# A decode step on one core: seven of V's eight chunks weighted on VectorE, the next queries ahead of its sums, the sum over V amid the next scores

## The chip, the cores and the metric

The kernel runs on 1 core of one Trainium2 chip. The core has a matrix engine (TensorE, PE in the profile), a vector engine (VectorE, DVE), a scalar engine (ScalarE, ACT), GpSimd (POOL) and SyncE (SP), which here only issues the transfers from the chip's main memory into the on-chip memory. TensorE writes to a separate memory of 8 banks (pS, pO and pK0 to pK5 in the code). The metric is the device time of one execution in microseconds, as the median over runs; less is better.

## The reference

Two kinds of layer alternate, attention over a cache (A) and a dense layer with GELU (B), for one query row `x` of 512 numbers, all in float32. The same caches and weights serve both passes.

```python
def _A_ref(x, k_cache, v_cache, wq, wo):            # H, Dh = 32, 128; 4096 keys
    q = (x @ wq).reshape(B, Sq, H, Dh).transpose(0, 2, 1, 3)
    scores = jnp.einsum("bhqd,bhkd->bhqk", q, k_cache) * (Dh ** -0.5)
    p = _softmax(scores, axis=-1)
    o = jnp.einsum("bhqk,bhkd->bhqd", p, v_cache)
    return o.transpose(0, 2, 1, 3).reshape(B, Sq, H * Dh) @ wo

def _B_ref(x, w1, b1, w2, b2):
    h = _gelu(jnp.einsum("bsd,df->bsf", x, w1) + b1)
    return jnp.einsum("bsf,fd->bsd", h, w2) + b2

x = x + _A_ref(_layernorm(x), k_cache, v_cache, wq, wo)
x = x + _B_ref(_layernorm(x), w1, b1, w2, b2)
x = x + _A_ref(_layernorm(x), k_cache, v_cache, wq, wo)
x = x + _B_ref(_layernorm(x), w1, b1, w2, b2)
```

## The kernel before, in words

The 32 heads are worked in G = 8 groups of J = 4 heads. Of one group, K and V are 8 MB each; both are cut into C = 8 chunks of 1 MB (one chunk is NC = 2048 numbers in each of 128 partitions, that is 512 for each of the four heads). The weights wq and wo of a group are 1 MB each and come as one transfer of 2 MB, the "pair" (wo of this group and wq of the next). The first pass goes through the groups 0 to 7; the second goes back from 6 (whose K and V, with 7's, are partly still on the chip) to 0. In the second pass the loop at L514 counts n from 2 to 7.

The on-chip memory holds one large tile, `arena`. Three "homes" of 8 MB each lie in it (A_AT, B_AT, C_AT); K and V of successive groups take them in turn, so that K of the next group goes where V of the group before lay, and V of the next group where K of this one lies. PAIR holds the pair, SCRATCH and TURNED short-lived results.

A group goes through these steps:

- `scores` (L222): for each chunk, four products of the queries z with K into pS, one for each head; each is two instructions in the profile, so a group's 32 products appear as x64.
- `exponentials` (L227): the maximum over pS (L228), the maximum over a head's rows through two small transposes (L230 to L233), the exponential on ScalarE (L237) with its sum.
- `weights` (L240): four transposes on TensorE, a copy to `pt` (L245), and the reciprocal of the sums (L251). `pt` and `rl` are the weights of V and 1 over their sum.
- V: `partly` (L407) lets TensorE take the first BY_PE = 3 chunks (`values`, L254, products into pO), and `weighted` (L261) lets VectorE take the other five: one multiplication of all five chunks by their weights in place (L265, 10240 numbers per partition), and additions that fold them onto one chunk (L270: 4096, 2048 and 2048 numbers).
- The next group's queries, `next_queries` (L379): the product of wq with x into pS, four transposes on VectorE (`turned`, L169), the queries z with the mean taken off (L218), and a memset of pS (L384).
- `group` (L393) begins with what the group before left "ahead": `sum_up` (L274) adds the folded chunk into pO by four products with ones, `head` (L278) picks the heads' results out of pO and scales them (L280, L284, L288). Then come this group's scores, and behind them `out_product` (L298), the product of the head with wo from PAIR into pO, which is added to the running sum of x behind the exponentials' first steps (`turned` at L404, `add_up` at L389).

Groups 0 to 5 of the first pass and n = 2 to 6 of the second give chunks to VectorE: 11 multiplications in all. In the last group of a pass, and in group 6 of the first, TensorE takes all eight chunks.

What sets the order: every transfer from SP, every product on TensorE, and the transposes on TensorE are pinned with `tc.keep_in_program_order`, so each of these queues runs in the order of the code. VectorE's instructions are not pinned; a planner places them when it takes them to be ready. SP issues, in order, K of a group, V, and the pair, and waits at each until the place that it writes has been read. So the pair waits for the product with wo of the group before, and K and V of the next group stand behind it. A few helpers record all instructions of a kind, so all loads have line L107 and all products L111; they are told apart by their tiles and shapes.

The mean of a layernorm is made by `minus_mean` (L189): a sum per partition is multiplied by a column of -1/512, in four products of 32 columns each, one for each quarter of the partitions. It is called twice (mean, variance) in each of the four layernorms. The dense layer (`mlp`, L307) streams w1 and w2 in pieces. In the last group of the second pass (L517 to L533) the code loads wo, w1 and w2 behind V; w1 goes to A_AT, where V of the group n = 6 lay.

Of the kernel before, what the change touches and what calls it, by code (L numbers as in the profile page):

```python
# [14 lines left out]
ALU = mybir.AluOpType  # L15
AX = mybir.AxisListType

P = 128
# [4 lines left out]
J = 4  # L23
C = 8
# [5 lines left out]
NC = 4 * U  # L30
# [13 lines left out]
TURNED = SHARED + 9 * U  # L44
ARENA = KEPT_K + 2 * U
HALVES = ((0, 4), (4, 8))
BY_PE = 3
ZQ = C - 1 + J * C
WIDE = 32 * J + 8 + 3 + 1
FRONT = 192  # L50
# [8 lines left out]
def decode_layers(ctx: ExitStack, tc: tile.TileContext, vectors, k, v, w, w1, w2, out):  # L59
    nc = tc.nc  # L60
# [21 lines left out]
    def small(name, n=1):  # L82
        nonlocal first_front, rest
        if name.startswith("gelu_"):
            i = "huaztg".index(name[-1])
            return cells[:, gelu + FB * i : gelu + FB * (i + 1)]
        if name not in places:
            fit = [j for j in range(J) if gaps[j] + n <= ends[j]]
            if name == "by_dma":
                places[name] = front, first_front, n  # L90
                first_front += n
            elif fit:
                places[name] = cells, gaps[fit[0]], n
                gaps[fit[0]] += n
            else:
                places[name] = cells, rest, n
                rest += n
        t, a, m = places[name]
        assert m == n and first_front <= FRONT and rest <= CELLS
        return t[:, a : a + n]  # L100

    def at(first, n):
        return arena[:, first : first + n]
# [6 lines left out]
    def matmul(*a, **kw):  # L110
        tc.keep_in_program_order(nc.tensor.matmul(*a, **kw))  # L111
# [10 lines left out]
    def by_four(t):  # L122
        return t.rearrange("p (j n) -> p j n", j=4)
# [10 lines left out]
    negmean = small("negmean")  # L134
# [8 lines left out]
    pS, pO = (psum.tile([P, 512], F32, name=n) for n in ("pS", "pO"))  # L143
# [19 lines left out]
    def turned(src, wide=False, to=None):  # L163

        t = turned_at[0] if to is None else to
        if wide:
            for j in range(J):
                q = slice(32 * j, 32 * j + 32)
                nc.vector.transpose(t[q], src[q, P * j : P * (j + 1)])  # L169
        else:  # L170
            nc.vector.transpose(t, src[:, :P])  # L171
        return t
# [14 lines left out]
        matmul(to[:, :n], zero[:, 0:1].to_broadcast([P, P]), at(of, n), start=not amid, stop=not amid)  # L187

    def minus_mean(s, at):  # L189
        for j in range(J):  # L190
            matmul(at[32 * j : 32 * j + 32, :], negmean.to_broadcast([P, 32]), s, start=True, stop=True)
        return at

    def mean_of(xs, s):
# [27 lines left out]
    def scores(z, c, kt):  # L222
        for j in range(J):
            matmul(pS[32 * j : 32 * j + C, :], z[:, C * j + C - 1 - c : C * j + 2 * C - 1 - c], kt[j],
                   start=(c == 0), stop=(c == C - 1))
# [32 lines left out]

    def weighted(pt, home):  # L261
        first = home + NC * BY_PE
        t = at(first, NC * (C - BY_PE)).rearrange("p (n d) -> p n d", d=P)
        w = pt.rearrange("p c j b -> p (c j b)")[:, 4 * J * BY_PE :]
        nc.vector.tensor_tensor(t, t, w.unsqueeze(2).to_broadcast([P, 4 * J * (C - BY_PE), P]), op=ALU.mult)  # L265
        n = C - BY_PE
        while n > 1:
            m = n // 2
            a, b = at(first + NC * (n - 2 * m), NC * m), at(first + NC * (n - m), NC * m)
            nc.vector.tensor_tensor(a, a, b, op=ALU.add)  # L270
            n -= m
        return quarters(first)

    def sum_up(t):  # L274
        for j in range(J):
            matmul(pO[32 * j : 32 * j + 4, :], one.to_broadcast([P, 4]), t[j], start=False, stop=True)

    def head(rl, last=False):  # L278
        ot = at(SCRATCH, U)
        nc.vector.transpose(ot, pO)  # L280
        o, on = small("o", 4), on_wide
        own = at(SCRATCH, 4 * 129).rearrange("p (b q) -> p b q", q=129)[:, :, :P]
        own = own.rearrange("p b (d q) -> p d b q", q=32)[:, :, :, 0]
        nc.vector.tensor_reduce(o, own, axis=AX.X, op=ALU.add)  # L284
        if last:
            nc.vector.tensor_scalar(on[:, :4], o, rl, None, op0=ALU.mult)
        else:
            nc.vector.tensor_scalar(in_quarters(on, 4), o.unsqueeze(1).to_broadcast([P, J, 4]), rl, None,  # L288
                                    op0=ALU.mult)
        return on  # L290
# [88 lines left out]
    def next_queries(xs, negm, wt, to=pO):  # L379
        for c in range(4):  # L380
            wide_query_block(to, c, xs, wt)
        z = queries(to, negm, wide=True)
        if to is pS:
            nc.vector.memset(pS, 0.0)  # L384
        return z
# [5 lines left out]


    def group(z, acc, ahead, k_blocks):  # L393
        if ahead:
            t, rl, wt = ahead
            sum_up(t)
            on = head(rl)
        for c, t in k_blocks:
            scores(z, c, t)
        if ahead:  # L400
            out_product(on, wt, pO)
        p = exponentials(sc, nsc)
        if ahead:
            acc = add_up(acc, of_32(turned(pO, wide=True), 4))  # L404
        return acc, *weights(p)

    def partly(pt, v_blocks, home):  # L407
        for c, t in v_blocks:
            if c < BY_PE:
                values(c, pt, t, c)  # L410
        return weighted(pt, home)


    negm, z, sc, nsc = first_queries(xs, s, wq_t, wide=True)
# [1 line left out]
    ahead = None  # L416
    for g in range(G):
        final = g == G - 1
        k_home, v_home = RING[2 * g % 3], RING[(2 * g + 1) % 3]
        acc, pt, rl = group(z, acc, ahead, blocks(k, g, k_home, HALVES if final else ((0, C),)))  # L420
        ahead = None
        if g == G - 2:
            nc.scalar.copy(at(KEPT_K, 2 * U), at(k_home + NC * C - 2 * U, 2 * U))
        if g < G - 2:
            t = partly(pt, blocks(v, g, v_home), v_home)
            pair = load(PAIR, of_w(g % 2, g, 2))
            ahead = t, rl, by_four(pair[:, :NC])
            z = next_queries(xs, negm, by_four(pair[:, NC:]), to=pS)
            continue
        for c, t in blocks(v, g, v_home, LAST if final else ((0, C),)):  # L430
            values(c, pt, t, c)
            if final and c in (5, 7):
                idle(pS)
            if g == G - 2:
                for j in range(J):
                    i = 4 * c + j - KEPT_V // U
                    if i >= 0:
                        nc.scalar.copy(pK[i], t[j])
        if final:
# [30 lines left out]
    xs, s = set_x(own, 0.5, xb)  # L470
# [4 lines left out]
    g = G - 2  # L475
# [12 lines left out]
    pair = load(C_AT + 24 * U, of_w(g % 2, g - 1, 2))  # L488
# [3 lines left out]
    p = exponentials(sc, nsc, lambda: queries(pO, negm, to=at(C_AT + 21 * U, P)))  # L492
    pt, rl = weights(p)
# [6 lines left out]
    for i, first in enumerate([SHARED, SHARED + U] + [PAIR + U * j for j in range(4)]):  # L500
        t = at(first, U)
# [4 lines left out]
    pt, rl = weights(exponentials(sc, nsc))  # L506
# [6 lines left out]
    homes, ahead = (A_AT, C_AT, B_AT), None  # L513
    for n in range(2, G):  # L514
        g, final = G - 1 - n, n == G - 1
        k_home, v_home = homes[(2 * n - 1) % 3], homes[2 * n % 3]
        acc, pt, rl = group(z, acc, ahead, blocks(k, g, k_home, HALVES if final else ((0, C),)))  # L517
        if not final:
            t = partly(pt, blocks(v, g, v_home, ((0, 6), (6, 8)) if n == 2 else ((0, C),)), v_home)
            pair = load(PAIR, of_w(g % 2, g - 1, 2))  # L520
            ahead = t, rl, by_four(pair[:, NC:])
            z = next_queries(xs, negm, by_four(pair[:, :NC]), to=pS)
            continue
        for c, t in blocks(v, g, v_home, LAST):
            values(c, pt, t, c)
            if c in (5, 7):
                idle(pS)
        wo_t = by_four(load(PAIR, of_w(g % 2, g, 1)))
        for a, b in W1_AT_END:
            load_w1(A_AT, a, b)  # L530
        for a, b in W2_AT_END:
            load_w2(A_AT + 11 * U, a, b)
        own = head_out(rl, wo_t, last=True)  # L533
# [46 lines left out]
```

## Time and profile before

| | |
|---|---|
| time, median of 3 runs | 672.79 us (672.41 to 673.16) |
| time of the profiled execution | 673.93 us |
| its span, from the first to the last instruction | 672.1 us |
| busy: PE / DVE / ACT | 400.7 / 329.1 / 22.8 us |
| the queue of the loads (q1) | 285.61 MB, 98.9% of 16 engines' span |
| mean granted clock of TensorE | 0.794 |

The profile is of one execution; what lies around its span, 1.8 us, is start and end of the program. In a row of the timeline stand the start in us, the duration in us, the engine, the line, the operation, the tile that it writes and the tile that it reads, a count where several were merged, and in brackets how long the engine had stood idle before it and what ended that. In a row of the groups stand the count, the busy time in us and the mean of one instruction in ns, then the idle time before them with what ended it. In a row of stretches stand the busy time of PE, of its weight load, of DVE, ACT and POOL, then the granted clock, the share of the DMA engines and GB/s. A merged row of DMA issues on SP covers the time from the first issue to the last; an issue does not tell when its data land, that shows at the instruction that waits for them.

### The profile page before, as it was taken

To read this page: it belongs to the slowest core of one execution; us is meant where nothing else is said; L and a number is where in the kernel's file an instruction comes from. 1 tells how busy PE (TensorE), PEld (TensorE's weight loads), DVE (VectorE), ACT (ScalarE), POOL (GpSimd) and SP (SyncE) were. 2 spreads that over 40 slices of the span, in tenths; PEclk is the share of its full clock that TensorE was granted. 3 is DMA by queue.
4 is the path that set the end of the run, shared out by engine and by line. 5 is a ranking of instruction groups with operands and counts; after the bars stand their busy time and mean duration, and the time that the engine had idled before them with its cause. 6 is when DMAs were issued, how large, how long until landed. Compare 5 with 4: busy or idle time off the path is not lost. (4 is left out here: it accounts for less than half of the span.)

```text
span 672.1 us, 5792 instructions
## 1 busy us (share of the span) xinstructions
PE 400.7 (60%) x2470; PEld 109.8 (16%) x2470; DVE 329.1 (49%) x480; ACT 22.8 (3%) x48; POOL 4.9 (1%) x23
## 2 busy tenths in 40 slices
PE   4543753647616556376767878728527466275685
PEld 1110210111201111011214222102102111021122
DVE  2059276393682945921121221492772936928521
ACT  0010000000000000002000110000000000000000
POOL 0000000000000000000000000000000000000000
PEclk9956765976769767677989999877758867687698
DMA  9999999999999999999999999999999999999996
GB/s 375 437 437 437 438 430 437 414 456 437 437 434 410 459 434 437 433 434 395 433 423 393 426 452 421 437 435 434 437 433 409 458 434 430 437 426 419 435 420 257
DMA packets 11258, 285.98 MB, mean 425 GB/s; under 512 B 1505, under 2 KB 1505, under 8 KB 3297
## 3 DMA queue, kind: packets, MB, share of 16 engines
q1 hardware_dynamic: 11088, 285.61, 98.9%
q8 instruction: 19, 0.31, 0.2%
q14 instruction: 7, 0.05, 0.0%
q10 hardware_dynamic: 144, 0.01, 0.0%
HBM read 285.62 MB, written 0.00 MB: 425 GB/s over the span
## 5 line engine op out<-in xcount | busy, mean ns | idle before, releaser
L111 PE MATMUL pO<-arena,cells 128*128 128x512 f32 (+4 forms) x376 | 93.0, 606 | 145.5 <-DVE arena L270 127.7
L111 PE MATMUL pS<-arena,front 128*8 128x512 f32 x1036 | 146.4, 706 | 32.8 <-DMA arena<-in_k 29.1
L265 DVE TENSOR_TENSOR arena<-arena 128x10240 f32<-128x10240 f32 x11 | 119.1, 10825 | 32.0 <-DMA arena<-in_v 31.8
L111 PE MATMUL pO<-arena 128*4 128x512 f32 x584 | 94.7, 806 | 44.7 <-DMA arena<-in_v 42.9
L270 DVE TENSOR_TENSOR arena<-arena 128x2048 f32<-128x2048 f32 (+1 forms) x33 | 98.5, 2985 | 0.7
L228 DVE TENSOR_REDUCE cells<-pS 128x1 f32<-128x512 f32 x16 | 11.1, 692 | 152.1 <-PE pS L111 152.1
L111 PEld LDWEIGHTS pO<-arena,cells 128*128 128x128 f32 (+3 forms) x376 | 28.2, 122 | 195.1 <-DVE arena L270 136.8
L111 PEld LDWEIGHTS pS<-arena,front 128*8 128x8 f32 x1036 | 31.4, 101 | 154.0 <-issue 110.3
L111 PE MATMUL pS<-arena,cells 128*1 128x128 f32 (+1 forms) x328 | 50.5, 384 | 8.5 <-DMA arena<-in_w 7.0
L280 DVE STREAM_TRANSPOSE arena<-pO 128x512 f32<-128x512 f32 x16 | 11.5, 717 | 54.1 <-PE pO L111 54.1
L242 PE MATMUL pO<-front,arena 128*128 128x128 f32 x64 | 12.8, 333 | 36.9 <-ACT arena L237 36.9
L111 PEld LDWEIGHTS pO<-arena 128*4 128x4 f32 x584 | 16.2, 102 | 107.7 <-issue 99.8
L169 DVE STREAM_TRANSPOSE arena<-pO 32x128 f32<-32x128 f32 x64 | 19.9, 311 | 20.1 <-PE pO L111 19.1
L237 ACT ACTIVATE arena<-pS,cells 128x512 f32<-128x512 f32 x16 | 12.4, 778 | 502.8 <-DVE cells L233 502.8
L111 PEld LDWEIGHTS pS<-arena,cells 128*1 128x1 f32 (+1 forms) x328 | 21.9, 118 | 45.2 <-issue 36.4
L231 DVE TENSOR_REDUCE cells<-cells 128x1 f32<-128x8 f32 x16 | 2.6, 161 | 29.4 <-PE pO L111 29.2
L242 PEld LDWEIGHTS pO<-front,arena 128*128 128x128 f32 x64 | 8.1, 161 | 49.9 <-ACT arena L237 48.8
L169 DVE STREAM_TRANSPOSE arena<-pS 32x128 f32<-32x128 f32 x44 | 13.7, 310 | 0.8
L171 DVE STREAM_TRANSPOSE arena<-pS 128x128 f32<-128x128 f32 x3 | 1.0, 317 | 12.7 <-PE pS L111 12.7
L247 DVE STREAM_TRANSPOSE cells<-cells 128x32 f32<-128x32 f32 x16 | 3.4, 214 | 7.0 <-ACT arena L237 5.9
L384 DVE MEMSET pS<- 128x512 f32 x11 | 5.3, 485 | 1.2
L245 DVE COPY arena<-pO 128x128 f32<-128x128 f32 x16 | 4.5, 284 | 1.4 <-PE pO L242 1.1
(63 smaller groups left out, 73.6 us busy)
## 6 DMA issues: line engine op xcount, KB each, us to landing
arena<-in_w SPq DMA_DIRECT2D x13, 2048.0 KB, 11.5
arena<-in_k SPq DMA_DIRECT2D x4, 4096.0 KB, 25.1
arena<-in_v SPq DMA_DIRECT2D x2, 4096.0 KB, 38.9
arena<-in_w SPq DMA_DIRECT2D x6, 1024.0 KB, 21.4
arena<-in_v SPq DMA_DIRECT2D x3, 2048.0 KB, 43.0
arena<-in_v SPq DMA_DIRECT2D x1, 6144.0 KB, 30.8
arena<-in_w SPq DMA_DIRECT2D x6, 688.0 KB, 30.3
arena<-in_v SPq DMA_DIRECT2D x4, 1024.0 KB, 46.2
```

The lines of the kernel that those rows point to most:

```text
L111: tc.keep_in_program_order(nc.tensor.matmul(*a, **kw))
L169: nc.vector.transpose(t[q], src[q, P * j : P * (j + 1)])
L228: nc.vector.tensor_reduce(ml[:, 0:1], pS, axis=AX.X, op=ALU.max)
L231: nc.vector.tensor_reduce(m, mt[:, :C], axis=AX.X, op=ALU.max)
L237: nc.scalar.activation(p, pS, AF.Exp, bias=bias[:, 0:1], scale=sc, accum_out=ml[:, 0:1])
L242: tc.keep_in_program_order(nc.tensor.transpose(pT[:, b].rearrange("p j r -> p (j r)"), p[:, P * b : P * (b + 1)], ident))
L245: nc.vector.tensor_copy(pt, pT[:, :, :, :C].rearrange("p b j c -> p c j b"))
L247: nc.vector.transpose(lt, ml)
L265: nc.vector.tensor_tensor(t, t, w.unsqueeze(2).to_broadcast([P, 4 * J * (C - BY_PE), P]), op=ALU.mult)
L270: nc.vector.tensor_tensor(a, a, b, op=ALU.add)
L280: nc.vector.transpose(ot, pO)
L384: nc.vector.memset(pS, 0.0)
```

## The change: what it does

Ten of the eleven groups that VectorE shares in leave one chunk to TensorE (BY_PE = 1) and give it seven; the first of the second pass (n = 2) keeps three for TensorE (BY_PE_AT_BEGIN). `weighted` is cut in two: the multiplication, and `added`, the additions. Between the two now stand the next group's queries, and the multiplication, the four transposes of pS and the additions are pinned in that order; z and the memset of pS are not. The sum over V and the head move from ahead of the scores to behind the sixth of their eight chunks. `minus_mean` makes one product with 128 columns instead of four with 32.

```diff
-BY_PE = 3
+BY_PE, BY_PE_AT_BEGIN = 1, 3
+SUM_BEHIND = 5
...
             for j in range(J):
                 q = slice(32 * j, 32 * j + 32)
-                nc.vector.transpose(t[q], src[q, P * j : P * (j + 1)])
+                turn = nc.vector.transpose(t[q], src[q, P * j : P * (j + 1)])
+                if src is pS:
+                    tc.keep_in_program_order(turn)
...
     def minus_mean(s, at):
-        for j in range(J):
-            matmul(at[32 * j : 32 * j + 32, :], negmean.to_broadcast([P, 32]), s, start=True, stop=True)
+        matmul(at, negmean.to_broadcast([P, P]), s, start=True, stop=True)
         return at
...
-    def weighted(pt, home):
-        first = home + NC * BY_PE
-        t = at(first, NC * (C - BY_PE)).rearrange("p (n d) -> p n d", d=P)
-        w = pt.rearrange("p c j b -> p (c j b)")[:, 4 * J * BY_PE :]
-        nc.vector.tensor_tensor(t, t, w.unsqueeze(2).to_broadcast([P, 4 * J * (C - BY_PE), P]), op=ALU.mult)
-        n = C - BY_PE
+    def pinned(*a, **kw):
+        tc.keep_in_program_order(nc.vector.tensor_tensor(*a, **kw))
+
+    def weighted(pt, home, by_pe):
+        t = at(home + NC * by_pe, NC * (C - by_pe)).rearrange("p (n d) -> p n d", d=P)
+        w = pt.rearrange("p c j b -> p (c j b)")[:, 4 * J * by_pe :]
+        pinned(t, t, w.unsqueeze(2).to_broadcast([P, 4 * J * (C - by_pe), P]), op=ALU.mult)
+
+    def added(home, by_pe=BY_PE):
+        first, n = home + NC * by_pe, C - by_pe
         while n > 1:
             m = n // 2
             a, b = at(first + NC * (n - 2 * m), NC * m), at(first + NC * (n - m), NC * m)
-            nc.vector.tensor_tensor(a, a, b, op=ALU.add)
+            pinned(a, a, b, op=ALU.add)
             n -= m
         return quarters(first)
...
     def group(z, acc, ahead, k_blocks):
-        if ahead:
-            t, rl, wt = ahead
-            sum_up(t)
-            on = head(rl)
         for c, t in k_blocks:
             scores(z, c, t)
+            if ahead and c == SUM_BEHIND:
+                t, rl, wt = ahead
+                sum_up(t)
+                on = head(rl)
         if ahead:
             out_product(on, wt, pO)
...
         if g < G - 2:
-            t = partly(pt, blocks(v, g, v_home), v_home)
+            partly(pt, blocks(v, g, v_home), v_home)
             pair = load(PAIR, of_w(g % 2, g, 2))
-            ahead = t, rl, by_four(pair[:, :NC])
             z = next_queries(xs, negm, by_four(pair[:, NC:]), to=pS)
+            ahead = added(v_home), rl, by_four(pair[:, :NC])
             continue
...
         if not final:
-            t = partly(pt, blocks(v, g, v_home, ((0, 6), (6, 8)) if n == 2 else ((0, C),)), v_home)
+            by_pe = BY_PE_AT_BEGIN if n == 2 else BY_PE
+            partly(pt, blocks(v, g, v_home, ((0, 6), (6, 8)) if n == 2 else ((0, C),)), v_home, by_pe)
             pair = load(PAIR, of_w(g % 2, g - 1, 2))
-            ahead = t, rl, by_four(pair[:, NC:])
             z = next_queries(xs, negm, by_four(pair[:, :NC]), to=pS)
+            ahead = added(v_home, by_pe), rl, by_four(pair[:, NC:])
             continue
```

`partly` passes `by_pe` on and no longer returns the folded chunk; `added` does.

More of the change, by code (lines that the diff above doesn't have):

```diff
@@ L405, in group, with partly @@
         return acc, *weights(p)
-    def partly(pt, v_blocks, home):
+    def partly(pt, v_blocks, home, by_pe=BY_PE):
         for c, t in v_blocks:
-            if c < BY_PE:
+            if c < by_pe:
                 values(c, pt, t, c)
-        return weighted(pt, home)
+        weighted(pt, home, by_pe)
     negm, z, sc, nsc = first_queries(xs, s, wq_t, wide=True)
```

## The prediction

> **What bounds the kernel now.** I read the page first: span, busy shares, the 40 slices, the DMA queue.
>
> ```profile
> span 672.1 us, 5792 instructions
> PE 400.7 (60%) x2470; PEld 109.8 (16%) x2470; DVE 329.1 (49%) x480; ACT 22.8 (3%) x48; POOL 4.9 (1%) x23
> GB/s 375 437 437 437 438 430 437 414 456 437 437 434 410 459 434 437 433 434 395 433 423 393 426 452 421 437 435 434 437 433 409 458 434 430 437 426 419 435 420 257
> q1 hardware_dynamic: 11088, 285.61, 98.9%
> ```
>
> No engine is above 60%, but the one queue that carries K, V and the weights keeps 16 engines busy for 98.9% of 672.1 us: 664.7. Only 7.4 us of engine time is unused, and the slices show where: the first (375 GB/s) and the last (257). In the timeline PE's last wait for weights ends at 666.94 (row below), 5.2 us before the end. So about 2 us are left for the start and the whole middle. The change moves no byte and does not touch the first load or the last step. It can gain almost nothing, and the question is whether it makes the queue run dry, or the end later.
>
> Second, the timeline of one steady group (V of group 1 lands at 89.35), and the tightest landing:
>
> ```profile
> 89.35 10.83 DVE L265 TENSOR_TENSOR arena<-arena 128x10240 f32<-128x10240 f32 x1 [3.82 <-DMA arena<-in_v]
> 109.74 1.89 PE L111 MATMUL pO<-arena,cells 128*4 128x512 f32 x8 [11.48 <-DVE arena L270]
> 111.70 0.72 DVE L280 STREAM_TRANSPOSE arena<-pO 128x512 f32<-128x512 f32 x1 [0.48 <-PE pO L111]
> 112.66 0.23 DVE L288 TENSOR_SCALAR cells<-cells 128x16 f32<-128x16 f32 x1
> 113.53 9.41 PE L111 MATMUL pS<-arena,front 128*8 128x512 f32 x64 [1.90 <-DMA arena<-in_k]
> 122.87 3.70 PE L111 MATMUL pO<-arena,cells 128*128 128x512 f32 x8
> 126.60 0.33 SPq L107 DMA_DIRECT2D arena<-in_w  x1
> 126.61 0.16 DVE L231 TENSOR_REDUCE cells<-cells 128x1 f32<-128x8 f32 x1 [2.65 <-PE pO L111]
> 127.46 0.42 SPq L107 DMA_DIRECT2D arena<-in_v  x1
> 129.78 0.15 DVE L251 RECIPROCAL cells<-cells 128x1 f32<-128x1 f32 x1
> 132.78 10.83 DVE L265 TENSOR_TENSOR arena<-arena 128x10240 f32<-128x10240 f32 x1 [2.84 <-DMA arena<-in_v]
> 176.22 10.83 DVE L265 TENSOR_TENSOR arena<-arena 128x10240 f32<-128x10240 f32 x1 [2.36 <-DMA arena<-in_v]
> ```
>
> V lands every 43.44 us (132.78 to 176.22). In that time pass 2 MB of w, 8 MB of K and 8 MB of V (18.87 million bytes): 434 GB/s, the rate of the full slices. Every stage waits for a landing: DVE for V (2.84 us; 2.36 in the tightest group), PE for K (1.90). SP sets the feed: w, K and V go out when the product over wo (122.87, 3.70) has read PAIR. At 126.60 the queue still holds V until 132.78, a reserve of 6.2 us. A late link has to eat 6.2 us on SP's side, or 2.36 us on VectorE's, before anything moves.
>
> **The change, part by part.** Durations come from the groups by shape:
>
> ```profile
> L265 DVE TENSOR_TENSOR arena<-arena 128x10240 f32<-128x10240 f32 x11 | 119.1, 10825 | 32.0 <-DMA arena<-in_v 31.8 <-DVE cells L251 0.2
> L270 DVE TENSOR_TENSOR arena<-arena 128x2048 f32<-128x2048 f32 x22 | 49.8, 2264 | 0.3
> L270 DVE TENSOR_TENSOR arena<-arena 128x4096 f32<-128x4096 f32 x11 | 48.7, 4425 | 0.4
> L169 DVE STREAM_TRANSPOSE arena<-pS 32x128 f32<-32x128 f32 x44 | 13.7, 310 | 0.8
> L384 DVE MEMSET pS<- 128x512 f32 x11 | 5.3, 485 | 1.2
> L218 DVE SCALAR_TENSOR_TENSOR front<-arena,cells 128x4 f32<-128x4 f32 x16 | 3.6, 225 | 0.5
> L111 PE MATMUL pS<-cells 128*32 128x1 f32 x64 | 1.9, 180 | 0.1
> ```
>
> *Seven chunks instead of five, in ten of the eleven groups.* From 4425 and 10825 ns, an element costs 1.042 ns and an instruction 0.16 us. The multiplication over 14336 elements is then 15.09 us (+4.27). The additions halve 7, 4, 2 chunks: 6144, 4096 and 2048 elements, 6.56 + 4.43 + 2.26 = 13.25 us (before: 4.43 + 2 x 2.26 = 8.95). DVE gains 8.6 us a group and PE loses eight of twelve value products. The PE time was spent while DVE multiplied, so dropping it frees nothing that anyone waits for.
>
> *Next queries first, sums behind, pinned.* Counted from V's landing: multiplication to 15.09, four transposes (4 x 0.31) to 16.33, z 0.23, memset of pS 0.49, sums 13.25: 30.3, with gaps 30.5. Before, the sums ended at 20.39 (109.74). The transposes need the product over wq, which PE finishes long before 15 us (below, 9.0 us after V in the last group). z and the memset are not pinned. The planner can place them straight behind the transposes (ready at 17.0) or behind the first addition (23.6). I think the second likelier, since it has let a ready instruction pass one that depends on its neighbour before: transposes sit between the dependent additions now. K lands at 24.18 (113.53), so either is in time, the second by 0.5 us.
>
> *Sum over V behind the sixth block of scores.* Scores start with K at 24.18 as now. A warm set of 64 takes 7.05 us (row below), so the last 16 take 1.76, and the first 48 end at 24.18 + 9.41 - 1.76 = 31.8. The sums are ready at 30.5: PE does not wait. The eight products cost 0.88 us warm (8/64 of 7.05), or 1.89 cold as at 109.74; PE has just run for 7 us, so I take 0.88: 32.7. Two blocks of scores follow to 34.5, and under them the head runs on DVE (111.70 to 112.89, 1.2 us) to 34.0. The product over wo goes from 34.5 to 38.2, against 37.2 now (126.57): **1.0 us later in each group**. If PE is cold for longer at the start of the scores, it may be 2.2; if shorter, 0.5 us earlier.
>
> What is queued behind it: on SP, w, K and V, with 6.2 us in hand; on DVE, L231 waits for that product (2.65) and with it exp and the weights, with 2.36 us in hand. Both cover 1.0. The loop on DVE itself closes in 38.2 + 3.4 (126.61 to 129.93) = 41.6 us, under 43.44. The queue stays full: **0 us in ten groups**. The group that keeps three chunks (n = 2) changes only in order: 0.
>
> *The last group (n = 7).* Here K comes in halves, nothing is loaded behind, and PE, not the queue, leads.
>
> ```profile
> 328.87 7.05 PE L111 MATMUL pS<-arena,front 128*8 128x512 f32 x64 [1.64 <-DVE front L218]
> 607.86 10.82 DVE L265 TENSOR_TENSOR arena<-arena 128x10240 f32<-128x10240 f32 x1 [3.18 <-DMA arena<-in_v]
> 613.13 3.75 PE L111 MATMUL pS<-arena,cells 128*128 128x512 f32 x8
> 629.91 8.95 PE L111 MATMUL pS<-arena,front 128*8 128x512 f32 x64
> 638.79 3.70 PE L111 MATMUL pO<-arena,cells 128*128 128x512 f32 x8
> 645.85 5.33 PE L111 MATMUL pO<-arena 128*4 128x512 f32 x48 [0.58 <-DVE arena L245]
> 660.63 0.76 PE L111 MATMUL pO<-arena,cells 128*2 128x344 f32 x8 [0.96 <-DMA arena<-in_w]
> 664.60 1.89 PE L111 MATMUL pS<-arena,cells 128*1 128x128 f32 x32 [2.16 <-DMA arena<-in_w]
> 666.94 2.24 PE L111 MATMUL pS<-arena,cells 128*1 128x128 f32 x56 [0.45 <-DMA arena<-in_w]
> ```
>
> The sums end at 607.86 + 30.5 = 638.4. Whether the scores start at 625 or 631.6, their first 48 are done by then, within a microsecond. Sum over V 638.4 to 639.3 (warm) and up to 641.0 with late scores, head 1.2, the product over wo about 641.9 to 645.6 against 638.79 to 642.49: **3.1 us later** (2.3 to 3.9). Exp, weights and V's 64 products follow without a wait (645.85 on), so the delay goes through to the dense layer. There PE waits for weights: 0.96 + 2.16 + 0.45 = 3.57 us that it can lose before the end moves. That cover holds 3.1 by half a microsecond: 0, at the far end 0.3 us. SP's loads of w1 now wait for the sum over V too (A_AT, chunk 1, is no longer PE's); issued at about 640, they are due behind V's last piece, some 10 us on.
>
> *Mean by one product.* Eight calls of eight instructions become two each (x64 to x16); a call took 0.22 us:
>
> ```profile
> 369.28 0.22 PE L111 MATMUL pS<-cells 128*32 128x1 f32 x8
> 371.92 3.76 SPq L107 DMA_DIRECT2D arena<-in_k  x3
> ```
>
> At two of eight, 0.06: 0.16 saved a call, at worst nothing if 128 weight columns load slower. Only between the passes can it count: the loads of K at 371.92 wait for scores behind that mean, and slice 22 (393 GB/s, 353 to 370 us) is low there, though smaller pieces load in it too. One or two calls lie on that path: -0.3 to 0, I take -0.1. Elsewhere a landing hides it.
>
> Sum: 0 in the groups, -0.1 between the passes, 0.1 at the end: 672.1 us of span, 673.93 us for the profiled run. That run lies 1.1 us above the median of the three shown, 672.79; on that scale **672.8 us**.
>
> **The rivals.** (1) *The last sum comes cold and shows at the end.* If z goes first, scores run from 625 to about 634 (K's second half lands near 632: 607.86 and 10.5 million bytes at 434 GB/s), and PE then stands still for 4.4 us until the sums. Such a pause can halve the clock:
>
> ```profile
> 89.39 5.24 PE L111 MATMUL pO<-arena 128*4 128x512 f32 x24 [4.26 <-DMA arena<-in_v]
> 88.00:96.00 8.00, 6.61 (x28) 1.47 (x29) 6.65 (x1) 0.00 (x0) 0.00 (x0) 0.60 1.08 463
> ```
>
> After 4.26 us without a matmul the stretch ran at 0.60. Sum over V, 16 scores and the product over wo are 0.88 + 1.76 + 3.70 = 6.3 us warm; half of them or all cold, 9.5 to 12.7. From 638.4 that ends at 647.9 to 651.1, 5.4 to 8.6 later, and 3.57 are covered: 1.8 to 5.0 slower, about 675. It decides from a delay of 3.57 us. Against it: one stretch does not tell how much of its low clock this pause made, and late scores (my likelier case) leave no pause. [...] Chance 0.12.
>
> (2) *z and the memset fall behind all sums* (or the pinning does not hold, and the transposes do). Then scores start at 30.5 instead of 24.18, the product over wo ends at 30.5 + 9.4 + 0.9 + 3.7 = 44.5, the next multiplication can start at 47.9, 4.5 us past 43.44. Over ten groups: some 45 us, 718. For it: nothing pins the two. Against: they are ready as soon as the transposes are. Chance 0.05.
>
> (3) *Faster.* A shorter mean closes the gap between the passes and the tail by more than I count: 7.4 us is all that the queue has unused, most of it start and end; 671.2. Chance 0.04.
>
> **How the numbers follow.** Forecast 0.79, rivals 0.12, 0.05, 0.04. About 0.2% (1.3 us) is what a measurement can tell from no change. The forecast's own span is 672.4 to 673.2, with the runs' spread 672.0 to 673.6. The lower end of rival 1 (1.8) brings the range to 674.6. Faster 0.04, same 0.79, slower 0.17.
>
> **What would show it.** Right: queue share near 98.9%; multiplications of about 15.1 us that still start on a DMA wait, 43.4 us apart; the wait of DVE for V about 1 us shorter; the product over wo in the last group ending near 645.6; the waits for weights in the last dense layer shrunk from 3.57 us to about half a microsecond, and the last 56 products still starting near 667. Wrong: a multiplication released by DVE L251 in the steady groups, a clock of 0.5 at the last sum, or those 56 starting after 668.

## The result and the profile after

The changed kernel takes 677.6 us (median of 6 runs, 674.98 to 679.34), the kernel before beside it 672.85 (6 runs, 672.41 to 673.98). The ratio is 1.0066, with a 95% interval of 1.0046 to 1.0087: slower by 0.66%, where no change was forecast. The profiled execution took 674.98 us, the shortest of its six, while that of before (673.93) lies near the top of its own. So these two traces stand only 1.1 us apart, and the experiments have to show the rest.

The page after: the span, busy time, the throughput in 40 slices, the load queue.

```profile
span 673.2 us, 5387 instructions
PE 380.3 (56%) x2262; PEld 112.8 (17%) x2262; DVE 415.5 (62%) x480; ACT 22.8 (3%) x48; POOL 4.9 (1%) x23
GB/s 374 436 436 436 437 437 436 416 454 433 432 436 411 459 436 425 436 433 420 436 407 394 424 445 423 442 432 429 436 436 411 461 433 425 428 423 438 429 415 238
q1 hardware_dynamic: 11088, 285.61, 98.8%
```

VectorE has 86 us more, PE 20 less, and the queue is as full as before. Next the steady group whose V lands at 89.07, and the next two starts of the multiplication:

```profile
89.07 15.09 DVE L264 TENSOR_TENSOR arena<-arena 128x14336 f32<-128x14336 f32 x1 [3.88 <-DMA arena<-in_v]
113.26 6.86 PE L112 MATMUL pS<-arena,front 128*8 128x512 f32 x48 [12.98 <-DMA arena<-in_k]
119.94 1.04 PE L112 MATMUL pO<-arena,cells 128*4 128x512 f32 x8
122.62 3.70 PE L112 MATMUL pO<-arena,cells 128*128 128x512 f32 x8
132.67 15.09 DVE L264 TENSOR_TENSOR arena<-arena 128x14336 f32<-128x14336 f32 x1 [2.97 <-DMA arena<-in_v]
176.28 15.09 DVE L264 TENSOR_TENSOR arena<-arena 128x14336 f32<-128x14336 f32 x1 [2.61 <-DMA arena<-in_v]
```

Every multiplication still waits for its V, 43.6 us apart. PE still waits for K, and the sum over V (119.94) follows the 48 scores without a wait. The product over wo starts 33.55 us after V's landing; before it was 33.52: the later sums do not make this group later. The wait for V is not 1 us shorter, as the prediction's list of signs had it, since the product over wo is not later.

The last group of the second pass, same columns:

```profile
607.34 15.09 DVE L264 TENSOR_TENSOR arena<-arena 128x14336 f32<-128x14336 f32 x1 [3.01 <-DMA arena<-in_v]
624.20 0.48 DVE L390 MEMSET pS<- 128x512 f32 x1
624.59 13.33 DVE L264 TENSOR_TENSOR arena<-arena 128x6144 f32<-128x6144 f32 x3
624.74 5.40 PE L112 MATMUL pS<-arena,front 128*8 128x512 f32 x32 [5.90 <-DVE pS L390]
632.31 1.90 PE L112 MATMUL pS<-arena,front 128*8 128x512 f32 x16 [2.17 <-DMA arena<-in_k]
637.98 1.31 PE L112 MATMUL pO<-arena,cells 128*4 128x512 f32 x8 [3.76 <-DVE arena L264]
639.04 3.39 PE L112 MATMUL pS<-arena,front 128*8 128x512 f32 x16
642.36 3.70 PE L112 MATMUL pO<-arena,cells 128*128 128x512 f32 x8
649.42 6.72 PE L112 MATMUL pO<-arena 128*4 128x512 f32 x48 [0.58 <-DVE arena L247]
662.09 0.76 PE L112 MATMUL pO<-arena,cells 128*2 128x344 f32 x8 [0.69 <-issue]
662.78 0.38 PE L112 MATMUL pS<-cells 128*128 128x1 f32 x2
667.65 2.58 PE L112 MATMUL pS<-arena,cells 128*1 128x128 f32 x88 [1.16 <-DVE cells L339]
```

The planner put z and the memset ahead of all three sums (624.20). So the scores start early, the six blocks that stand ahead of the sum over V are done by 634.2, and PE, which works in the order of the code, stands for 3.76 us until VectorE's sums end. Then the next 16 scores take 3.39 us, against 1.90 for the 16 at 632.31. The granted clock (the last number but two of a row) tells why:

```profile
632.31:634.21 1.90, 1.90 (x16) 0.34 (x16) 1.90 (x1) 0.00 (x0) 0.00 (x0) 1.00 0.88 379
639.04:642.36 3.32, 3.32 (x20) 0.53 (x13) 1.14 (x3) 0.00 (x0) 0.00 (x0) 0.55 0.92 395
```

Products at a granted clock near a half are called cold below, at 1.00 warm. The product over wo starts 35.02 us after V's landing (607.34); before it was 30.93: 4.09 us later. V's next 48 products take 6.72 us instead of 5.33. The dense layer begins at 662.09, and its last 88 products run in one go behind an engine (1.16, DVE): the three waits for weights of before, 3.57 us, are all gone.

The chain that ended last tells it the same way. Before:

```profile
646.71 20.18 DMA arena<-in_w
666.94 2.28 PE pS L111 x56
```

and after:

```profile
637.98 1.31 PE pO L112 x8
649.42 6.72 PE pO L112 x48
667.65 2.63 PE pS L112 x88
```

The end was set by the weights' transfer; now it is set by work, from the sums on. In all the last product ends 62.89 us after V's landing (670.23 less 607.34), before 61.32 (669.18 less 607.86): 1.57 us of this pair of traces come from the last group.

### The profile page after: what moved, and what is told of

Same layout as the page of the kernel before. It is cut to its first block, busy times and chain, and to the rows that moved or that the text cites. A ratio compares the mean times of both kernels' runs of the same rounds, so it can differ in the third digit from the quotient of the medians.

```text
span 673.2 us, 5387 instructions
## 1 busy us (share of the span) xinstructions
PE 380.3 (56%) x2262; PEld 112.8 (17%) x2262; DVE 415.5 (62%) x480; ACT 22.8 (3%) x48; POOL 4.9 (1%) x23
## 3 DMA queue, kind: packets, MB, share of 16 engines
q1 hardware_dynamic: 11088, 285.61, 98.8%
## 5 line engine op out<-in xcount | busy, mean ns | idle before, releaser
L264 DVE TENSOR_TENSOR arena<-arena 128x2048 f32<-128x2048 f32 (+4 forms) x44 | 303.3, 6894 | 27.3 <-DMA arena<-in_v 26.6
L112 PE MATMUL pO<-arena,cells 128*128 128x512 f32 (+4 forms) x376 | 82.2, 499 | 19.9 <-POOL cells L186 6.6
L112 PE MATMUL pS<-arena,cells 128*1 128x128 f32 (+1 forms) x328 | 72.5, 441 | 33.8 <-DMA arena<-in_w 31.3
L112 PE MATMUL pO<-arena 128*4 128x512 f32 x424 | 66.2, 766 | 40.7 <-DMA arena<-in_v 38.8
L112 PEld LDWEIGHTS pS<-arena,cells 128*1 128x1 f32 (+1 forms) x328 | 30.2, 140 | 87.4 <-issue 78.3
L244 PE MATMUL pO<-front,arena 128*128 128x128 f32 x64 | 10.9, 295 | 36.9 <-ACT arena L239 36.9
L112 PEld LDWEIGHTS pO<-arena 128*4 128x4 f32 x424 | 10.4, 93 | 76.7 <-issue 72.6
L112 PE MATMUL pO<-arena,front 128*128 128x128 f32 (+2 forms) x18 | 5.1, 382 | 0.0
## 6 DMA issues: line engine op xcount, KB each, us to landing
arena<-in_v SPq DMA_DIRECT2D x2, 4096.0 KB, 39.2
```

The lines of the kernel that those rows point to most:

```text
L244: tc.keep_in_program_order(nc.tensor.transpose(pT[:, b].rearrange("p j r -> p (j r)"), p[:, P * b : P * (b + 1)], ident))
L264: tc.keep_in_program_order(nc.vector.tensor_tensor(*a, **kw))
```

## The experiments

Three theories. **A:** the last group is late by more than the weights' waits can cover, partly since PE goes cold in its pause. **B:** VectorE's longer work costs something in every group. **C:** the mean by one product costs time where PE leads. e1 to e4 ran on one chip, e5 to e15 on another; each is compared with the kernel before on the same chip. The times first (us; the ratio is to the kernel before):

| run | V's chunks by PE ahead of the last group | mean by | median | ratio, 95% |
|---|---|---|---|---|
| changed kernel | 1 | one product | 677.6 | 1.0046 to 1.0087 |
| e7, the same again | 1 | one product | 676.4 | 1.0035 to 1.0060 |
| e3 | 1 | four products | 674.55 | 1.0007 to 1.0030 |
| e1 | 3 | one product | 674.39 | 1.0000 to 1.0025 |
| e11, e1 again | 3 | one product | 674.21 | 1.0006 to 1.0025 |
| e5 | 3 | four products | 672.59 | 0.9984 to 1.0002 |
| e12, e5 again | 3 | four products | 672.99 | 0.9985 to 1.0004 |
| e6 (kernel before) | 3 | one product | 672.53 | 0.9980 to 0.9998 |

### e1 and e11: three of V's chunks by PE ahead of the last group

```diff
-            by_pe = BY_PE_AT_BEGIN if n == 2 else BY_PE
+            by_pe = BY_PE_AT_BEGIN if n in (2, G - 2) else BY_PE
```

> The changed kernel, but the group before the last one (n = 6) keeps three chunks for TensorE as before; the other nine groups keep seven chunks on VectorE. Theory A (the loss arises in the last group alone: the sums of seven chunks end at about 638, TensorE stands still for them, cools, and what follows shows at the end): the sums end near 630 again, the product over wo ends by about 643 and the time is back at that of the kernel before, 672.4 to 673.4 (ratio 0.9995 to 1.001). Theory B (the longer VectorE work of every group costs, through its loop or the loads): nine tenths of the loss stay, 676 to 678. Theory C (the mean by one product costs): no change from the changed kernel, 677 to 678.

The last group of e1:

```profile
610.37 4.19 PE L112 MATMUL pO<-arena 128*4 128x512 f32 x24 [2.43 <-DMA arena<-in_v]
637.51 1.03 PE L112 MATMUL pO<-arena,cells 128*4 128x512 f32 x8
640.19 3.70 PE L112 MATMUL pO<-arena,cells 128*128 128x512 f32 x8
667.83 3.12 PE L112 MATMUL pS<-arena,cells 128*1 128x128 f32 x56 [0.84 <-DMA arena<-in_w]
```

The sum over V comes without a pause, the product over wo 29.8 us after V's landing (610.37), and at the end PE waits for weights again. The time falls by 2.0 us against e7 and 3.2 against the first measurement: A has a part. But 674.39 lies above A's 672.4 to 673.4, and e11 repeats it:

> e1 unaltered, one product in all eight calls: if the cost of the one product is real, 674.4 as before (1.0012 to 1.0025 of the kernel before); if it was chance of chip and batch, 672.6.

It took 674.21 us. So something else costs 1 to 2 us.

### e2: four products without a use ahead of the last sum, to keep PE warm

```diff
+                for _ in range(4 if last else 0):
+                    idle(pK[0])
                 sum_up(t)
```

> The changed kernel with four extra products of zeros (128 x 512 each, into a bank that nothing reads) between the sixth block of scores and the sum over V, in the last group of the second pass alone. They change no result. Theory A with the clock as its larger half: TensorE no longer stands still for 3.8 us, so the sum, the last two blocks of scores, the product over wo and V's products run at full clock: 673 to 674. Theory A with lateness alone (the sums end at 638 whatever the clock): at most 1 us better, 676 to 677.5. Theories B and C: 677 to 678.

It took 675.04 us (1.0014 to 1.0039), between the two forms of A. Its last group:

```profile
636.38 3.70 PE L112 MATMUL pK<-arena,front 128*128 128x512 f32 x8
641.07 1.90 PE L112 MATMUL pS<-arena,front 128*8 128x512 f32 x16
649.96 7.03 PE L112 MATMUL pO<-arena 128*4 128x512 f32 x48 [0.57 <-DVE arena L247]
668.50 2.58 PE L112 MATMUL pS<-arena,cells 128*1 128x128 f32 x88 [1.16 <-DVE cells L339]
```

The scores behind the filler are warm (1.90 instead of 3.39), so the pause had made them cold. V's 48 products come cold all the same, behind the next pause (7.03 us, against 5.33 in before). The median lies below both measurements of the changed kernel, but the interval meets that of e7 (from 1.0035): a gain in the expected direction, not a proven one.

### e3: the mean by four products again

```diff
-        matmul(at, negmean.to_broadcast([P, P]), s, start=True, stop=True)
+        for j in range(J):
+            matmul(at[32 * j : 32 * j + 32, :], negmean.to_broadcast([P, 32]), s, start=True, stop=True)
```

> The changed kernel with the mean made by four products of 32 columns again. In the profiles a call of one product took 0.38 us, one of four 0.22. Theory A: two calls lie on the late path behind the last group, so 0.2 to 0.5 us better, 677.0 to 677.6. Theory C (the single product of 128 columns is what costs, before the second pass and at the end): 673 to 674.

It took 674.55 us, between A's 677.0 and C's 674: the one product has a part in the loss, but not all of it. Two rows, of the last group and of one call in its dense layer:

```profile
637.11 1.89 PE L112 MATMUL pO<-arena,cells 128*4 128x512 f32 x8 [4.61 <-DVE arena L265]
661.37 0.22 PE L112 MATMUL pS<-cells 128*32 128x1 f32 x8
```

The last group is still late and cold (4.61 us of pause, and 1.89 for the sum), which leaves 1.0007 to 1.0030. A call in four products takes 0.22 us here as before; in one product it takes 0.38 (662.78 above).

### e4: in the last group the sum ahead of all scores

```diff
+        if last:
+            t, rl, wt = ahead
+            sum_up(t)
+            on = head(rl)
         for c, t in k_blocks:
             scores(z, c, t)
-            if ahead and c == SUM_BEHIND:
+            if ahead and c == SUM_BEHIND and not last:
```

> The changed kernel, but in the last group alone the sum over V and the head stand ahead of all scores again, while VectorE keeps seven chunks. Theory A: the whole set of scores now starts at about 639.5 instead of being three quarters done by then, 5 to 7 us more of the same delay on the same path: 681 to 685. Theories B and C: the last group has cover, no change within 1 us, 677 to 678.5.

It took 682.47 us (1.0114 to 1.0151), 9.5 more than the kernel before.

```profile
638.78 1.89 PE L112 MATMUL pO<-arena,cells 128*4 128x512 f32 x8 [20.60 <-DVE arena L264]
640.45 8.47 PE L112 MATMUL pS<-arena,front 128*8 128x512 f32 x64
648.85 3.70 PE L112 MATMUL pO<-arena,cells 128*128 128x512 f32 x8
```

The whole set of scores now stands behind the sums, and the product over wo starts 10.07 us after the sums' end (648.85 less 638.78) instead of 4.38 (642.36 less 637.98): 5.7 later. The time grows by 4.9 to 6.1 us over the two measurements of the changed kernel. With the waits for weights gone, nearly each microsecond in this group is one at the end.

### e5 and e12: e1 and e3 together

> The changed kernel with both suspects undone: three chunks for TensorE in the group before the last one, and the mean by four products. Nine groups still give seven chunks to VectorE, with the queries ahead of the sums and the sum amid the scores. Theory A+C (two separate costs, the late last group and the slower mean ahead of the second pass, each about 1.6 us by the two runs before): 672.5 to 673.3, the time of the kernel before. Theory B (the longer VectorE work of the nine groups has a cost of its own): 674 or more.

It took 672.59 us. Seven chunks on VectorE in nine groups, the pinned order and the sum amid the scores are still in it, and it equals the kernel before within 0.2%. **B falls.** And e3, which differs from it in the last group's split alone, lies clear above it (from 1.0007 against up to 1.0002): **A is shown.** The traces agree. From the landing of the last V to the end of the last product pass 59.96 to 61.47 us in the eleven traces in which the group ahead keeps three chunks (the kernel before among them), and 61.91, 62.89 and 63.24 in the three that give seven in the changed kernel's order with nothing to fill the pause (e3, the changed kernel, e7). The repeat on another occasion:

> e5 unaltered: 672.6, equal to the kernel before within 0.2%, by every theory; more than 674 would say that e5's time was chance.

672.99 us, again equal. The table's terms add: e3 is 2.0 us above e5, e1 is 1.8 above it, and 672.59 + 2.0 + 1.8 = 676.4, what e7 took. By the ratios, since e3 and e1 ran on the other chip, they give 1.0038, inside e7's interval. So A and C account for the loss as e7 has it; the first measurement (from 1.0046) lies above that, and the 1.2 us between the two are not explained.

### e6 and e14: the kernel before with one product

> The kernel before with only the mean by one product of 128 columns. Theory C: the call costs 0.15 us more, several of them follow one another between the passes where the queue of loads runs short, and the time rises by 0.8 to 2 us: 673.7 to 675. Theory A alone (the mean does not matter): 672.7 to 673.1. A gain (672.5 or less) would mean that fewer instructions are worth something after all.

The diff is e3's turned round, in the kernel before. It took 672.53 us, no slower than the kernel before (0.9980 to 0.9998), and again:

> The kernel before with one product for the mean, unaltered from e6: 672.5, no slower than the kernel before, if the one product costs nothing there. If that was chance, 674 or more, and the one product costs 1 to 2 us in every order.

672.41 us (0.9977 to 0.9994). In the order of before, the one product costs nothing, and C as it was put here (673.7 to 675) falls. So C is no price of its own: it needs something else in the change.

### e7 and e8: the changed kernel again, and a warm last group

> The changed kernel unaltered, beside the others on one chip, for its time there and a second profile. Theory A+C: about 676 (672.9 and twice 1.6), up to 677.7 if the two costs help each other. In the profile the last group's sums end 30.5 us after V lands and the product over wo ends 38 to 39 us after it; the stretch from 365 to 395 us loses 1 us or more against the kernel before.

It took 676.4 us (5 runs): the loss repeats, a little smaller. The trace (675.29, the shortest of the five) has the late last group, with the sums ending 30.6 us and the product over wo 39.2 us after V's landing. It has no loss between the passes: the second pass's scores start at 370.59, in before at 370.81. The last V lands at 607.29 here, at 607.34 in the other trace of the changed kernel, and at 607.86 in before. So the loss that C stands for shows in neither trace of the changed kernel, both of them of short runs.

> The changed kernel with the mean by four products, and with extra products of zeros in the last group of the second pass: four ahead of the sum over V and two behind the product over wo, so that TensorE hardly stands still there. They change no result. Without them this kernel took 674.55. Theory A by the clock: sum, product over wo and V's products run at full clock, 672.7 to 673.5. Theory A by lateness: the extra products add nothing and gain little, 674 to 675.

```diff
+                for _ in range(4 if last else 0):
+                    idle(pK[0])
                 sum_up(t)
...
             out_product(on, wt, pO)
+        for _ in range(2 if last else 0):
+            idle(pK[0])
```

e8 is e3 with these products without a use around the last sum. It took 673.82 us (1.0004 to 1.0023) against e3's 674.55 (1.0007 to 1.0030): the right direction again, but between the two forecasts, and again the intervals overlap. Its 48 products ran warm (5.33 us), and took 6.20 us in e3. The last group of e8, and the first and the last row of e3's:

```profile
609.26 15.09 DVE L265 TENSOR_TENSOR arena<-arena 128x14336 f32<-128x14336 f32 x1 [2.68 <-DMA arena<-in_v]
642.58 3.70 PE L112 MATMUL pO<-arena,cells 128*128 128x512 f32 x8
649.64 5.33 PE L112 MATMUL pO<-arena 128*4 128x512 f32 x48 [0.57 <-DVE arena L248]
665.95 3.11 PE L112 MATMUL pS<-arena,cells 128*1 128x128 f32 x88 [1.16 <-DVE cells L340]
```

```profile
606.48 15.09 DVE L265 TENSOR_TENSOR arena<-arena 128x14336 f32<-128x14336 f32 x1 [1.79 <-DMA arena<-in_v]
665.81 2.58 PE L112 MATMUL pS<-arena,cells 128*1 128x128 f32 x88 [1.16 <-DVE cells L340]
```

No wait for weights is left at the end of e8, and yet its last product ends only 59.80 us after V's landing (669.06 less 609.26), against 61.91 in e3 (668.39 less 606.48) and 61.32 in before. So in this trace the lateness, 2.17 us at the start of the dense layer (51.66 us after V against 49.49), is covered, and the cold clock is what e3 loses in its last group. What e8's trace has above before came earlier: its last V lands 2.78 us later than e3's, with the same code up to there.

### e9 and e10: where does the one product cost?

Both are e5 with one product in some of the calls of `minus_mean` alone: in the four from the first dense layer to the second pass's scores (e9, below), or in the last two (e10, `len(calls) > 6`).

```diff
+        calls.append(at)
+        if 2 <= len(calls) - 1 < 6:
+            matmul(at, negmean.to_broadcast([P, P]), s, start=True, stop=True)
+            return at
         for j in range(J):
```

> The kernel e5 (three of V's chunks by PE before the last group, four products for the mean), with one product for the mean in the four calls from the first dense layer to the scores of the second pass alone. The theory that the 1.8 us that the one product costs in the changed order arise between the passes, where loads and PE release each other in turn, expects 674.4 (e5 had 672.6) and scores of the second pass that start 1 to 1.6 us later than e5's 370.45. The rival, that it is the tail, expects 672.6. A third, that the 1.8 us are chance of two chips and batches, expects 672.6 to 673 here and in the other three.

> The kernel e5 with one product for the mean in the two calls of the last dense layer alone. The theory of the tail expects 674.4, at most: the two calls take 0.38 instead of 0.22 us each, 0.3 us by their own time. The theory of the stretch between the passes expects 672.6; the last group is not late here and weights are waited for behind the calls, so 672.6 is also what the trace of e5 lets expect. Chance: 672.6 to 673.

e10 took 672.41 us (0.9985 to 1.0002): nothing at the end, where the last group is in time. e9 took 673.36 (0.9991 to 1.0022, single runs up to 677.44): 0.4 above e12 on the same chip, neither the 1.8 nor nothing. In its trace the second pass's scores start at 369.97, not 1 to 1.6 us behind e5's 370.45, but that is one of its shorter runs (672.27). So the end is ruled out where the last group is in time, and the place between the passes is neither shown nor excluded. The two calls ahead of the first group were not tried alone.

### e13 and e15: what makes the one product costly?

```diff
-BY_PE, BY_PE_AT_BEGIN = 1, 3
+BY_PE, BY_PE_AT_BEGIN = 3, 3
```

> The changed kernel with three of V's chunks by PE in every group: the pinned order, the sum over V amid the scores and the mean by one product are left, the seven chunks are gone. Measured so far: with seven chunks in nine groups, three in the last, one product costs 1.2 and 1.8 us (674.21 against 672.99, 674.39 against 672.59), and nothing in the kernel before (672.53 against 673.0). If the seven chunks make the one product costly (each group, or the entry into the first dense layer, comes later), this gives 672.6. If the moved sum or the pinned order does, it gives 674.3.

e13 (this diff, in the changed kernel) took 673.26 us (0.9990 to 1.0015): the same median as the kernel before beside it, though between the two forecasts. Order and moved sum do not cost the whole 1.2 to 1.8 us; the interval leaves room for a part (1.0 us). e15 is e1 with three chunks by PE ahead of the end of the first pass as well:

```diff
-            partly(pt, blocks(v, g, v_home), v_home)
+            by_pe = BY_PE_AT_BEGIN if g == G - 3 else BY_PE
+            partly(pt, blocks(v, g, v_home), v_home, by_pe)
...
-            ahead = added(v_home), rl, by_four(pair[:, :NC])
+            ahead = added(v_home, by_pe), rl, by_four(pair[:, :NC])
```

> e1 (three chunks by PE ahead of the last group, one product), with three chunks by PE also in the last group of the first pass that gives chunks to VectorE. If what makes the one product costly is a late entry into the stretch between the passes, as the late last group made the end late, this gives 672.6 and scores of the second pass that start near 370.5; if not, 674.3.

e15 took 672.57 us (0.9980 to 1.0000), with the one product in all eight calls and seven chunks in eight groups. So the seven chunks are costly in two places, ahead of the end of each pass, and only the first pass's needs the one product to show. How it does so, the traces do not show. The second call of the mean between the passes, in e11 and in e15:

```profile
371.01 0.38 PE L112 MATMUL pS<-cells 128*128 128x1 f32 x2
```

```profile
369.69 0.38 PE L112 MATMUL pS<-cells 128*128 128x1 f32 x2
```

and in e3 and in e8, which are the same code up to the last group:

```profile
368.66 0.24 PE L112 MATMUL pS<-cells 128*32 128x1 f32 x8
```

```profile
370.22 0.24 PE L112 MATMUL pS<-cells 128*32 128x1 f32 x8
```

The call comes 1.32 us later in e11 than in e15, but e3 and e8 lie 1.56 apart, so one trace of each cannot show a cost of this size. Nor is the end of the first pass seen to be late: in every trace PE waits for V of its last two groups, the last time for 2.31 us in e11 and 2.55 in e15, and that V lands at the same 341.2 in both. That the seven chunks there are needed is shown by e15's time; by what way they make the one product costly stays open.

## Why the prediction was wrong, step by step

**What bounds the kernel, and the middle groups: right.** The queue is 98.8% busy (98.9% forecast), multiplications take 15.09 us (15.09), and DVE's wait for V persists in each steady group. The product over wo comes no later than before, where 1.0 us was forecast: the 48 scores took 6.86 us, where 7.65 were reckoned. e5 and e12 show that these groups cost nothing. VectorE's additions in the last group end 30.6 us after V (30.5 forecast).

**The last group: this step failed.** The prediction took z and the memset to fall behind the first addition, and a product over wo 3.1 us late, "That cover holds 3.1 by half a microsecond: 0". z came first, as rival 1 had it; PE stood 3.76 us, the scores behind were cold, and the product came 4.09 us late. With V's 48 products cold (1.39 more) the dense layer began 5.26 us later after V's landing than in the row of before:

```profile
657.35 0.76 PE L111 MATMUL pO<-arena,cells 128*2 128x344 f32 x8 [0.91 <-POOL cells L309]
```

(657.35 less 607.86 is 49.49, 662.09 less 607.34 is 54.75). Of this 3.57 are covered, 1.7 show, and 1.57 were measured at the end. By e8, where these products ran warm, a delay of 2.17 us is covered as the prediction reckoned: it was the pause and the cold clock, taken as absent, that broke the step. Rival 1 gave 1.8 to 5.0 us, about 675: its mechanism (0.55 behind a pause of 3.76 us) and its point of decision held, and by itself (e3 against before) it costs 1.6 us by the medians. Its sizes did not: it had the product over wo 5.4 to 8.6 us late, with that product partly cold, but this ran warm (3.70), and V's 48 products, which it left out, ran cold. Its chance of 0.12 was the error. It rested on a guess at the planner, which the order of before gave no row for.

**A cover used to its last half microsecond is not one.** V's 48 products stand behind the same pause in the traces named here: 3.36 us from the end of the product over wo, with only four short transposes in it. They took 5.33 us in before, e5 and e11, 6.72 in the changed kernel, and 7.03 in e2; and 7.03 also in e15, whose last group is in time:

```profile
645.81 7.03 PE L112 MATMUL pO<-arena 128*4 128x512 f32 x48 [0.57 <-DVE arena L247]
666.22 2.90 PE L112 MATMUL pS<-arena,cells 128*1 128x128 f32 x56 [0.82 <-DMA arena<-in_w]
```

There the 1.7 us are taken out of the waits for weights, and one wait is left. So the 3.57 us that the prediction meant to spend on a delay were already in part the reserve for a cold start that comes in some runs and not in others. Why the same 3.36 us were followed by 5.33 us in some traces and by 7.03 in others, no run here shows.

**Mean by one product: wrong in sign.** The forecast was 0.06 us a call; it is 0.38 against 0.22. The instructions fell to a quarter, but each loads 128 weight columns instead of 32. The groups of weight loads, after and then before (mean ns of one in the second place behind the bar):

```profile
L112 PEld LDWEIGHTS pS<-cells 128*128 128x128 f32 x16 | 2.8, 206 | 4.3 <-issue 2.9 <-DVE cells L200 1.4
```

```profile
L111 PEld LDWEIGHTS pS<-cells 128*32 128x32 f32 x64 | 1.7, 117 | 5.1 <-issue 4.0 <-DVE cells L198 1.1
```

A call takes about as long as two such loads, 2 x 206 ns. Eight loads of 117 ns would take 0.94 us one after another, and the eight instructions took 0.22, so the narrow ones overlap. That the loads set the time of a call is argued from these numbers, not shown by a run. The prediction had named this case ("at worst nothing if 128 weight columns load slower") and bounded it at zero, with no reason that excluded a loss. That -0.1 us between the passes was a cost of 0 in the order of before (e6, e14), and of 1.2 to 1.8 us with seven chunks up to the end of the first pass (e1 and e11 against e5 and e12).

**The ten groups, "0 us in ten groups":** right for eight. The group ahead of the end of the first pass was counted among them, and e15 shows that it costs 1.6 us together with the one product. In the traces nothing behind it is seen to be late that would explain this, so why it does is not known.

**The range** ended at 674.6 since it took only the lower end of rival 1 in. Its upper end, 5.0, holds both measurements (4.75 and 3.4 above before), but for a further reason: 1.6 to 2.0 us of them are rival 1 (e3 against before and against e5), and 1.2 to 1.8 come with the one product, a second loss that no part of the prediction had. What the first measurement has beyond these is not explained.

## What to carry to other kernels

Where one queue is full all the time, look apart at the stretches that are not like the middle groups (the end, a change of pass): work that was free in every middle group was paid there, and giving just the groups ahead of them the old split (e15) returned the whole loss. A cover is worth what it holds in the worst run, less what a cold clock takes out of it in some runs (1.7 us here), and two steps that spend the same cover must be added. When fewer, wider products replace narrow ones, price them by a measured call and not by the number of instructions: here a load of 128 columns took 206 ns in the mean, one of 32 took 117.

Nothing here beats the kernel before by more than the 0.2% that the prediction took for what a measurement can tell: e14, e6 and e15 lie 0.14, 0.11 and 0.10% below it.

## What the runs showed of the hardware

In the calls from the first dense layer on, four products of 32 weight columns, one for each quarter of the partitions, took 0.22 or 0.24 us together, and one of 128 columns took 0.38; in the two calls at the start it was 0.29 and 0.29 in before, 0.42 and 0.28 in the changed kernel. A pause of 3.36 us on PE, with four transposes of 0.66 us together in it, was followed by 48 products in 5.33 us in some traces and in 7.03 in others, by the same kernel too (e5 and its repeat e12, below). Over the first 3 us of these products the granted clock was 1.00 in before (5.33) and 0.53 in the changed kernel (6.72).

```profile
646.00 5.33 PE L112 MATMUL pO<-arena 128*4 128x512 f32 x48 [0.57 <-DVE arena L248]
```

```profile
645.45 7.03 PE L112 MATMUL pO<-arena 128*4 128x512 f32 x48 [0.57 <-DVE arena L248]
```

The runs of the changed kernel spread over 4.4 us, those of the kernel before over 1.6. The clock is one possible cause; another is that the last V lands at other times with the same code up to there, at 606.48 in e3 and at 609.26 in e8. Which of them makes the spread is not shown.
